# Second feed-forward part of an attention kernel as seven block products instead of eight

## The chip, the core and the metric

One core of a Trainium2 chip runs the whole program in one launch. The metric is the device time of that core in microseconds; the median of several runs counts. TensorE (PE in the profile) does the matrix products and accumulates them in PSUM, which has eight banks of 128 partitions by 512 float32. VectorE (DVE), ScalarE (ACT) and GpSimd (POOL) do the elementwise work, and SyncE (SP) issues every DMA. An engine works through its own instructions in order and waits for the others by semaphores.

## The reference, cut to what matters

```python
attn_out = _attn_ref(q, k, v, f)            # 4 batches, 8 heads, 576 tokens, head size 64
x = attn_out.transpose(0, 2, 1, 3).reshape(2304, 512)
x = square(maximum(x @ moe_w_in, 0)) @ moe_w_out         # first part:  512 -> 2048 -> 512
h = x @ moe2_w_in                                        # second part: 512 -> 2048
return (h - tanh(h)) @ moe2_w_out                        #              2048 -> 512
```

The attention has a causal mask and a decay. The weights arrive as float64 and are joined to float32 on the chip.

## The kernel before, in words

Attention and the first feed-forward part are interleaved on TensorE; the second part follows alone. All products of the feed-forward parts run on values split in two: a rounded high part in fp32r and a low part, the rest. One product of A and B is then three matmuls: high by high, low by high, high by low. A high part is a copy on ScalarE (`rounded`, L86), a low part a subtraction (`rest`, L100).

The first part goes through eight blocks of 288 tokens (TB, L48). For each of 16 feature tiles i, `h_step` (L131) does 12 matmuls (3 terms, 4 pieces of the contraction) into a bank, ScalarE applies Relu and two squares, and the low part is formed by the engine that the table ENG names (L155). `y_step` (L158) follows LAG = 2 steps later with 12 matmuls into four banks that hold the output of a block over all 16 steps. `y_out` (L697) splits the four banks into high and low, and stores both to y_d in DRAM (L75).

The second part uses the same two functions with ph = 2 on blocks of 512 tokens (TB2, L49): four of 512 and one of 256 (BLK, L728). Per step: 12 matmuls of 512 columns, Tanh on ScalarE (L152), the difference on DVE (L153), the high part on ScalarE (L154), the low part on DVE (L155), then 12 matmuls of `y_step`. `load_x` (L730) fetches a block's high and low from y_d, `out_emit` (L716) copies the result out of PSUM and stores it. `h_step` has one bank (psh, L172) until the last two blocks of the first part, when attention is over; from there it has three (psh2, L780).

Weights of the second part: `fetch_w` (L106) loads a half tile (512 KB as float64), `split_w` (L113) joins the two words on ScalarE and DVE (L120 to L122) and splits into high and low. `w2_split` (L762) spreads the 32 half tiles over the last two blocks of the first part and the first blocks of the second (W2_AT, L750). High and low then stay in SBUF; nothing of the weights goes back to DRAM. GpSimd has no work in this stretch.

The order of the instructions: the program is built twice. In the first stretch, up to MARK (block 2 of the first part, L771), each engine keeps the order of the first build (L815 to L823). Behind it the order comes from a scheduler that takes instructions by simulated time. The main loop is L769 to L812.

Of the kernel before, what the change touches and what calls it, by code (L numbers as in the profile page):

```python
# [48 lines left out]
TB2 = 512  # L49
# [4 lines left out]
def kernel(  # L54
# [76 lines left out]
    def h_step(ph, i, x, psh, n, j):  # L131
        xh, xl = x
        wh, wl = (W[ph, i, 0][:, a] for a in range(2))
        ps = psh.tile([128, 512], F32, tag="h", name="hp")[:, :n]
        ops = [(w, x, k) for w, x in ((wh, xh), (wl, xh), (wh, xl)) for k in range(NK)]
        for jj, (w, x, k) in enumerate(ops):
            xk = x[:, k] if ph == 1 else x[k // 2][:, k % 2]
            nc.tensor.matmul(ps, w[:, k * 128:(k + 1) * 128], xk, start=(jj == 0), stop=(jj == 11))  # L138
        if ph == 1:
            tmp = f1.tile([128, TB], F32, tag="tmp", bufs=2, name="tmp")  # L140
            gh = f1.tile([128, TB], F32R, tag="gh", bufs=RING, name="gh")
            gl = f1.tile([128, TB], F32R, tag="gl", bufs=RING, name="gl")
        else:
            tmp = late.tile([128, TB2], F32, tag="tmp", name="tmp", bufs=2)[:, :n]
            ghl = f1.tile([128, 4 * TB], F32R, tag="xhl", bufs=4, name="ghl")
            gh, gl = ghl[:, :n], ghl[:, TB2:TB2 + n]
        if ph == 1:
            nc.scalar.activation(tmp, ps, AF.Relu)  # L148
            nc.scalar.activation(gh, tmp, AF.Square)  # L149
            nc.scalar.activation(tmp, tmp, AF.Square)  # L150
        else:
            nc.scalar.activation(tmp, ps, AF.Tanh)  # L152
            nc.vector.tensor_tensor(tmp, ps, tmp, ALU.subtract)  # L153
            rounded(nc.scalar, gh, tmp)  # L154
        rest(by("gl7" if j == NB - 1 else "gl" if j < 2 else "l_gl") if ph == 1 else nc.vector, gl, tmp, gh)  # L155
# [717 lines left out]
```

## Time and profile before

| what | us |
|---|---|
| median of 3 runs | 1088.02 (1087.4 to 1090.89) |
| span of the profiled execution, first to last instruction | 1079.7 |
| TensorE busy | 1029.2 |
| VectorE busy | 594.0 |
| ScalarE busy | 524.7 |
| GpSimd busy | 250.6 |

The profile gives the profiled execution by its span; a time of its own beside it is not listed. Median less span is 8.3 us, the time around the program. Busy time of TensorE is modelled: neighbouring matmuls overlap, so the mean of one matmul (some 300 ns) is longer than the distance from one start to the next, and it is the distance that adds up to the time. "PEld" is TensorE's weight load, one for each matmul. A windows row gives, for a stretch, its length, the busy time and the number of instructions of each engine, the granted clock of TensorE, the busy share of the DMA engines and their rate.

### The profile page before, as it was taken

What the parts mean: (1) busy time and instruction counts of PE and PEld (TensorE: products, weight loads), DVE (VectorE), ACT (ScalarE), POOL (GpSimd) and SP (SyncE); (2) the same over time, 40 slices, a digit from 0 to 9 for tenths busy, and PEclk for the clock granted to TensorE, in tenths of its full rate; (3) what the DMA queues carried; (4) which work ended last, traced back from release to release, by engine and by line L of the source; (5) the groups of instructions that cost most, each with busy time, mean ns of one, the idle gap of its engine ahead of it and who ended that gap; (6) DMA issues with size and microseconds to landing.
All of it is one profiled execution on the core that took longest, in us unless ns stands there. A gap on an engine that the chain in (4) does not pass through costs nothing.

```text
span 1079.7 us, 16821 instructions
## 1 busy us (share of the span) xinstructions
PE 1029.2 (95%) x6048; PEld 898.8 (83%) x6048; DVE 594.0 (55%) x1566; ACT 524.7 (49%) x1221; POOL 250.6 (23%) x358
## 2 busy tenths in 40 slices
PE   4899999999999898999999999999999999999998
PEld 3577678888998888888889999888888888888898
DVE  5887777768787767877525545642222322222232
ACT  6977677665556446455436667432222222222232
POOL 4244455555353442534210000000000000000000
PEclk9989999999999899999989999999999999999999
DMA  7657643225955658745646088100200300110010
GB/s 243 199 138 213 185 140 136 89 82 174 293 180 171 195 154 253 258 141 162 184 161 228 2 305 285 45 1 25 92 1 1 117 1 1 39 40 1 1 40 21
DMA packets 63301, 134.83 MB, mean 125 GB/s; under 512 B 6416, under 2 KB 31568, under 8 KB 61168
## 3 DMA queue, kind: packets, MB, share of 16 engines
q1 hardware_dynamic: 63216, 133.74, 38.9%
q8 instruction: 48, 0.79, 0.3%
q14 instruction: 37, 0.30, 0.1%
HBM read 93.94 MB, written 39.78 MB: 124 GB/s over the span
## 4 chain that ended last, share of the span: by engine, by line
PE 75%; DMA 11%; DVE 6%; POOL 2%; issue 2%; SPq 2%; ACT 2%; POOLq 0%; ACTq 0%; DVEq 0%
PE hp L138 32%; PE yp L164 32%; DMA PTl<-p_d 6%; PE o_ps L552 3%; DMA p_d<-T 3%; PE o_ps L367 2%; DVE PTl L101 2%; PE s_ps L476 1%; SPq L518 1%; DVE P L443 1%; PE s_ps L477 1%; DMA raw<-in_w_dram 1%; POOL PTh L90 1%; PE s_ps L326 1%; PE t_ps L487 1%
## 5 line engine op out<-in xcount | busy, mean ns | idle before, releaser
L138 PE MATMUL hp<-xhl,w 128*128 128x288 f32 (+2 forms) x2496 | 454.2, 329 | 2.5 <-ACT tmp L148 1.7
L138 PEld LDWEIGHTS hp<-xhl,w 128*128 128x128 f32 x2496 | 388.8, 192 | 41.0 <-issue 2.7
L164 PE MATMUL yp<-ghl,w 128*128 128x512 f32 (+1 forms) x960 | 216.0, 374 | 0.0
L164 PE MATMUL yp<-gh,w 128*128 128x288 f32 x1024 | 200.9, 301 | 0.0
L164 PEld LDWEIGHTS yp<-ghl,w 128*128 128x128 f32 x960 | 168.4, 188 | 34.5
L153 DVE TENSOR_TENSOR tmp<-hp,tmp 128x512 f32<-128x512 f32 (+1 forms) x80 | 51.0, 638 | 209.8 <-ACT tmp L152 209.8
L164 PEld LDWEIGHTS yp<-gh,w 128*128 128x128 f32 x1024 | 161.9, 191 | 1.6 <-issue 0.4
L152 ACT ACTIVATE tmp<-hp 128x512 f32<-128x512 f32 (+1 forms) x80 | 44.4, 555 | 225.0 <-PE hp L138 224.8
L164 PE MATMUL yp<-gl,w 128*128 128x288 f32 x512 | 133.5, 299 | 2.6 <-DVE gl L101 1.5
L148 ACT ACTIVATE tmp<-hp 128x288 f32<-128x288 f32 x128 | 51.9, 407 | 121.6 <-PE hp L138 118.4
L452 ACT ACTIVATE P<-P,ST 128x320 f32<-128x320 f32 (+4 forms) x151 | 84.6, 561 | 39.5 <-DVE ST L443 38.2
L164 PEld LDWEIGHTS yp<-gl,w 128*128 128x128 f32 x512 | 90.4, 190 | 5.0 <-DVE gl L101 2.3
L463 POOL TENSOR_SCALAR P<-P,ST 128x448 f32<-128x448 f32 (+4 forms) x88 | 58.4, 666 | 93.3 <-DVE ST L457 52.3
L101 DVE TENSOR_TENSOR ghl<-tmp,ghl 128x512 fp32r<-128x512 f32 (+1 forms) x80 | 51.1, 639 | 49.2 <-ACT ghl L88 49.2
L443 DVE CUSTOM_DVE_ANT_0 P<-s_ps,mk 128x320 f32<-128x320 f32 (+3 forms) x151 | 63.6, 433 | 25.2 <-PE s_ps L477 12.0
L101 DVE TENSOR_TENSOR gl<-tmp,gh 128x288 fp32r<-128x288 f32 x96 | 48.4, 505 | 47.2 <-ACT tmp L150 46.6
L101 DVE TENSOR_TENSOR PTl<-PTl,PTh 128x512 fp32r<-128x512 f32 (+1 forms) x64 | 51.9, 841 | 39.4 <-POOL PTh L90 39.3
L88 ACT ACTIVATE ghl<-tmp 128x512 fp32r<-128x512 f32 (+1 forms) x80 | 47.2, 590 | 49.9 <-DVE tmp L153 49.8
L101 DVE TENSOR_TENSOR w<-wst,w 128x512 fp32r<-128x512 f32 x64 | 46.1, 725 | 28.9 <-ACT w L88 28.6
L90 POOL TENSOR_SCALAR PTh<-PTl 128x512 fp32r<-128x512 f32 (+1 forms) x64 | 46.3, 750 | 59.8 <-DMA PTl<-p_d 59.0
L149 ACT ACTIVATE gh<-tmp 128x288 fp32r<-128x288 f32 x128 | 56.5, 443 | 4.1 <-PE yp L164 1.2
L150 ACT ACTIVATE tmp<-tmp 128x288 f32<-128x288 f32 x128 | 56.0, 438 | 2.1
(122 smaller groups left out, 1187.7 us busy)
## 6 DMA issues: line engine op xcount, KB each, us to landing
raw<-in_w_dram SPq DMA_DIRECT2D x64, 512.0 KB
p_d<-T SPq DMA_DIRECT2D x16, 1024.0 KB
PTl<-p_d SPq DMA_DIRECT2D x64, 256.0 KB
R<-in_qk_dram SPq DMA_DIRECT2D x24, 576.0 KB
xhl<-y_d SPq DMA_DIRECT2D x16, 512.0 KB
xhl<-x_d SPq DMA_DIRECT2D x14, 576.0 KB
y_d<-yst SPq DMA_DIRECT2D x14, 576.0 KB
VR<-in_v_dram SPq DMA_DIRECT2D x32, 160.0 KB
```

Of the source, the lines that this page charges most:

```text
L88: eng.activation(out, in_, AF.Copy)
L90: eng.tensor_scalar(out, in_, 1.0, 1.0, ALU.mult, ALU.mult)
L101: eng.tensor_tensor(out, in_, hi.bitcast(F32), ALU.subtract)
L138: nc.tensor.matmul(ps, w[:, k * 128:(k + 1) * 128], xk, start=(jj == 0), stop=(jj == 11))
L148: nc.scalar.activation(tmp, ps, AF.Relu)
L149: nc.scalar.activation(gh, tmp, AF.Square)
L150: nc.scalar.activation(tmp, tmp, AF.Square)
L153: nc.vector.tensor_tensor(tmp, ps, tmp, ALU.subtract)
L164: nc.tensor.matmul(yp[m][:, :n], w[:, c], x, start=(i == 0 and j == 0), stop=(i == NF - 1 and j == 2))
L443: nc.vector.tensor_tensor_reduce(p[:rows, a:b], ps[:rows, :b - a], mk[:rows, o:o + b - a], -0.125, 3.0e38 if mn is None else mn, ALU.add, ...
L452: nc.scalar.activation(p[:rows, :n], p[:rows, :n], AF.Exp, bias=mn, scale=-1.0, accum_out=st[:rows, 1, t:t + 1])
L463: by(n_by).tensor_scalar(p[:rows, :n], p[:rows, :n], st[:rows, 3, t:t + 1], 1.0, ALU.mult, ALU.mult)
```

## The change

The second part is cut into 2 by 2 blocks and done by Strassen's scheme: seven products P1 to P7 of sums of blocks instead of eight products of blocks. The sums of the weights (S1 to S4) and of the activations (T1 to T4) are formed on DVE, split in high and low, and each of the seven products is again three matmuls.

- **h products.** A group g is two feature tiles (8 groups); a batch b is 576 tokens as two halves of 288 (N2). The loop of 32 steps n does P6, P1, P7, P5 of step n, then P2, P4, P3 of step n-1: 42 matmuls of 288 columns. Partial sums are formed in place: DVE adds to banks in PSUM, and P2, P4 and P3 accumulate on what is there. Four Tanh and four differences per step, one of the differences on GpSimd ("c22"). The result g_d goes to DRAM as float32 (590 KB a step).
- **y products.** Four rounds of 512 tokens. In each the seven accumulators stay in seven banks over all eight groups: 42 matmuls of 256 columns a group. `y_evict` combines the seven once a round, on DVE. The last 256 tokens go by the plain eight products (`y_rest`, 192 matmuls of 256 columns).
- **Weights.** `prep_all` joins, sums and splits a group's w_in (s = 0) during the last two blocks of the first part, at the steps PREPS, and stores high and low of seven blocks to wg_d in DRAM (1.84 MB a group; groups 6 and 7 stay in SBUF). `w_load` brings them back. w_out (s = 1) is prepared during the h loop (PREP2_AT). Low parts of w2 ("w2_lo") and of the h products' operands ("xo_lo") are on GpSimd; those of the y products stay on DVE.
- **Memory.** Weights of the first part move to pools that are closed one after another in its last block, and the new pools pa0 to pa3 open in their place. In the last two blocks `h_step` keeps the single bank psh; psh2 now belongs to the second part. `y_out` only copies out of PSUM, two banks on ScalarE and two on DVE, and y_d holds one float32 in place of two.
- **Order.** Everything of the second part is chained in the order in which it is written, on each engine.

```diff
--- before.py
+++ after.py
+    "w2_lo": "P", "xo_lo": "P", "c22": "P",
...
-TB2 = 512
+NG = NF // 2
+N2 = 288
+NQ = 256
+NYB = NTOK // (2 * NQ)
+PREPS = (((6, 1), 0, 0), ((6, 3), 0, 1), ((6, 6), 0, 2), ((6, 8), 0, 3), ((6, 11), 0, 4), ((6, 13), 0, 5),
+         ((7, 1), 1, 0), ((7, 6), 0, 6), ((7, 10), 0, 7))
+PREP2_AT = (None, 2, 6, 10, 14, 18, 25, 28)
+DIRECT = {(0, 6): 0, (0, 7): 1, (1, 6): 4, (1, 7): 6}
+HOME_G = ({6: 0, 7: 1, 0: 2, 1: 3, 2: 4, 3: 5, 4: 6, 5: 7}, {0: 2, 1: 3, 6: 4, 2: 5, 7: 6, 3: 7, 4: 0, 5: 1})
+YSEQ = (0, 6, 1, 7, 2, 3, 4, 5)
...
+    y_d = dram.tile([NK, 128, NTOK], F32, name="y_d")
+    g_d = [dram.tile([128, 2, NTOK], F32, name=f"g_d{g}") for g in range(NG)]
+    wg_d = [[dram.tile([128, 2, 7 + s, 256], F32, name=f"wg_d{s}_{g}") for g in range(NG)] for s in range(2)]
...
+    def prep_fetch(s, g):
+        raw = WRAW[s, g] = late.tile([128, 2, 1024], U32 if WIDE else F32, tag="raw", name="raw")
+        for n, a in enumerate(((1, 0), (0, 1))[s]):
+            src = w2[2 * g + a][:, s * 512:(s + 1) * 512]
+            nc.sync.dma_start(raw[:, n] if WIDE else raw[:, n, :512], src.bitcast(U32) if WIDE else src)
...
+    def prep_sum(s, g, name):
+        q = {k: WT[s, g][:, i] for k, i in (SLOT[s] | SUMS).items()}
+        a, b, op = WSUM[name]
+        nc.vector.tensor_tensor(q[name], q[a], q[b], op)
...
+    def prep_lo(s, g, a, b):
...
+        t = WT[s, g][:, a:b]
+        rest(by("w2_lo"), t, t, WH[s, g][:, a:b])
...
+        src = WT[s, g] if which else WH[s, g].bitcast(F32)
+        o = 1 - s
+        nc.sync.dma_start(wg_d[s][g][:, which, a - o:b - o], src[:, a:b])
...
+    def prep_all(s, g):
+        with tc.issue_after(latest(EngineType.DVE)):
+            for n in range(2):
+                prep_wide(s, g, n)
+                prep_shift(s, g, n)
+                prep_or(s, g, n)
+            for k in ("S1", "S3", "S2", "S4"):
+                prep_sum(s, g, k)
+            cuts_ = (1 - s, 2, 4, 6, 8)
+            for a, b in zip(cuts_, cuts_[1:]):
+                prep_hi(s, g, a, b)
+                prep_lo(s, g, a, b)
+            for which in range(2):
+                prep_store(s, g, which, 1 - s, 8)
...
+    def w_load(s, g):
+        hl = home(s, g)
...
+            nc.sync.dma_start(hl[:, a].bitcast(F32), wg_d[s][g][:, a, s:])
+        place(s, g, hl)
...
+    def x_op(b, names):
+        for n in names:
+            xo = x_out(b, n)
+            rounded(nc.scalar, xo[:, 0], XT[b, n])
+            rest(by("xo_lo"), xo[:, 1], XT[b, n], xo[:, 0])
...
+                psh2 = ctx.enter_context(tc.tile_pool(name="psh2", bufs=1, space=bass.MemoryType.PSUM))
...
+                G[g] = h_step(i, X[j], psh, TB, j)
+            for k, (at, *which) in enumerate(PREPS):
+                if (j, i) == at:
+                    prep_all(*which)
+                    prep_fetch(*(PREPS[k + 1][1:] if k + 1 < len(PREPS) else (1, 1)))
...
+        if jy == NB - 1 and iy % 4 == 3 and iy < 15:
+            early[iy // 4].close()
+            pa.append(ctx.enter_context(tc.tile_pool(name=f"pa{iy // 4}", bufs=1)))
+            if iy == 3:
+                x_load(0)
+                x_sum(0, ("T1", "T2", "T3", "T4"))
+            elif iy == 7:
+                x_op(0, ("T2", "B11", "T3", "T1", "B21", "T4", "B22"))
+            else:
+                w_load(0, 0)
+                w_load(0, 1)
...
+    TERMS = ((0, 0), (1, 0), (0, 1))
+    FACTORS = {"P1": ("A11", "B11"), "P2": ("A12", "B21"), "P3": ("S4", "B22"), "P4": ("A22", "T4"),
+               "P5": ("S1", "T1"), "P6": ("S2", "T2"), "P7": ("S3", "T3")}
+    HOME = {"P1": 0, "P2": 0, "P6": 1, "P7": 2, "P4": 2, "P5": 3, "P3": 3}
+    RING7 = [(0, i) for i in (1, 2, 3)] + [(1, i) for i in range(4)]
...
+    def h_prod(n, p):
+        b, g = divmod(n, NG)
+        wn, xn = FACTORS[p]
+        wg, xo = WG[0, g][wn], XO[b, xn]
+        ps = BK[n][HOME[p]]
+        first_ = p in ("P6", "P1", "P7", "P5")
+        for i, (ws, xs, k) in enumerate([(ws, xs, k) for ws, xs in TERMS for k in range(2)]):
+            nc.tensor.matmul(ps, wg[:, ws, k * 128:(k + 1) * 128], xo[:, xs, k],
+                             start=(i == 0 and first_), stop=(i == 5), skip_group_check=True)
+    def h_act(n, k):
+        src = BK[n][(0, 2, 3)[k]]
+        q = (1, 3, 0)[k]
+        nc.scalar.activation(TH[:, k], src, AF.Tanh)
+        nc.vector.tensor_tensor(GQ[n][:, q], src, TH[:, k], ALU.subtract)
...
+    def y_sum(n):
+        if n >= REST:
+            return
+        B12, B11, B22, B21, T1, T2, T3, T4 = (GT[n][:, i] for i in range(8))
+        for o, x, y in ((T1, B12, B11), (T3, B22, B12), (T2, B22, T1), (T4, B21, T2)):
...
+        rounded(nc.scalar, YO[n][0], GT[n][:, 8 - q:])
...
+        rest(nc.vector, YO[n][1], GT.pop(n)[:, 8 - q:], YO[n][0])
...
+    YORDER = ("P1", "P6", "P2", "P7", "P4", "P5", "P3")
+    def y_prod(n, p, acc):
+        i, g = n % NG, YSEQ[n % NG]
+        wn, xn = FACTORS[p]
+        wg = WG[1, g][wn]
+        for m in range(2):
+            ps = acc[p][:, m * NQ:(m + 1) * NQ]
+            for j, (ws, xs) in enumerate(TERMS):
+                nc.tensor.matmul(ps, wg[:, ws, m * 128:(m + 1) * 128], YO[n][xs][:, YX[xn]],
+                                 start=(j == 0 and m == 0 and i == 0), stop=(j == 2 and i == NG - 1), skip_group_check=True)
...
+        nc.scalar.activation(cp, v["P1"], AF.Copy)
+        add(u2, v["P6"], cp)
+        add(o1[:, :, 1], v["P2"], cp)
+        add(x, v["P7"], u2)
+        add(o2[:, :, 1], v["P4"], x)
+        add(z, v["P5"], u2)
+        add(o2[:, :, 0], v["P5"], x)
+        nc.sync.dma_start(out[0:2, :, t:t + 2 * NQ].rearrange("k p n -> p k n"), o2.rearrange("p m a n -> p m (a n)"))
+        add(o1[:, :, 0], v["P3"], z)
+        nc.sync.dma_start(out[2:4, :, t:t + 2 * NQ].rearrange("k p n -> p k n"), o1.rearrange("p m a n -> p m (a n)"))
...
+    XOP_AT = {4: ("B11",), 6: ("T2",), 7: ("B21",)}
+    TSUM_AT = {4: ("T1", "T3"), 5: ("T2", "T4")}
+    YLOAD_AT = {25: 0, 26: 1, 28: 2, 30: 3, 31: 4}
...
+        x = [bank2(*RING7[(3 * n + i) % 7])[:, :N2] for i in range(3)]
+        BK[n] = [x[0], bank2(0, 0)[:, :N2], x[1], x[2]]
...
+        if n < 3:
+            w_load(0, n + 3)
+        if g == 3 and b + 1 < B:
+            x_load(b + 1)
...
+        for p in ("P6", "P1", "P7", "P5"):
+            h_prod(n, p)
+        nc.scalar.activation(cp, BK[n][0], AF.Copy)
+        nc.vector.tensor_tensor(uv, BK[n][1], cp, ALU.add)
+        if g == NG - 1 and b + 1 < B:
+            x_op(b + 1, ("T3",))
+        nc.vector.tensor_tensor(BK[n][2], BK[n][2], uv, ALU.add)
...
+        nc.vector.tensor_tensor(c22, BK[n][3], xc, ALU.add)
+        nc.vector.tensor_tensor(BK[n][3], BK[n][3], uv, ALU.add)
...
+            GQ[n - 1] = late.tile([128, 4, N2], F32, tag="gq", bufs=2, name="gq")
+            h_prod(n - 1, "P2")
+            h_act(n - 1, 0)
...
+            nc.scalar.activation(TH[:, 3], SM[:, 6 + (n - 1) % 2], AF.Tanh)
+            by("c22").tensor_tensor(GQ[n - 1][:, 2], SM[:, 6 + (n - 1) % 2], TH[:, 3], ALU.subtract)
+            h_prod(n - 1, "P4")
+            h_act(n - 1, 1)
+            h_prod(n - 1, "P3")
+            h_act(n - 1, 2)
...
+                prep_hi(1, k, 0, 4)
+                prep_lo(1, k, 0, 2)
+                prep_lo(1, k, 2, 4)
...
+            h_store(n - 1)
...
+    for n in range(REST):
+        k, g = divmod(n, NG)
+        if g == 0:
+            if k:
+                keys, spare_key = [spare_key] + keys[:-1], keys[-1]
+            acc = {p: bank2(*key) for p, key in zip(YORDER, keys)}
+        for p in YORDER:
+            y_prod(n, p, acc)
+        y_load(n + 4)
+        if n == 1:
+            w_load(1, 5)
+        if n == 0:
...
+        y_rest(u, acc)
...
```

## Rows read from the trace of the kernel before

**Rows 1.** The page: span, busy time by engine, chain by engine and by line.

```profile
span 1079.7 us, 16821 instructions
PE 1029.2 (95%) x6048; PEld 898.8 (83%) x6048; DVE 594.0 (55%) x1566; ACT 524.7 (49%) x1221; POOL 250.6 (23%) x358
...
PE 75%; DMA 11%; DVE 6%; POOL 2%; issue 2%; SPq 2%; ACT 2%; POOLq 0%; ACTq 0%; DVEq 0%
```

**Rows 2.** Windows: the first part's last two blocks; from the first 512-column matmul on.

```profile
565.00:669.75 104.75, 104.75 (x790) 104.75 (x788) 54.20 (x107) 69.00 (x158) 0.00 (x0) 1.00 0.60 212
669.75:1079.70 409.95, 405.89 (x1946) 337.68 (x1944) 127.34 (x206) 109.37 (x194) 0.00 (x0) 1.00 0.08 29
```

**Rows 3.** Timeline of PE: start, length of the group, matmul, count; 512 columns.

```profile
669.75 2.93 PE L138 MATMUL hp<-xhl,w 128*128 128x512 f32 x12
...
689.55 2.92 PE L138 MATMUL hp<-xhl,w 128*128 128x512 f32 x12
...
695.12 2.92 PE L138 MATMUL hp<-xhl,w 128*128 128x512 f32 x12
```

**Rows 4.** Timeline of PE: 288 columns, with 12 of y_step between the two.

```profile
663.36 1.76 PE L138 MATMUL hp<-xhl,w 128*128 128x288 f32 x12
...
666.55 1.76 PE L138 MATMUL hp<-xhl,w 128*128 128x288 f32 x12
```

**Rows 5.** Timeline of PE: 256 columns, 276 matmuls from the first start to the last group's.

```profile
1038.12 1.59 PE L138 MATMUL hp<-xhl,w 128*128 128x256 f32 x12
...
1071.15 4.48 PE L164 MATMUL yp<-ghl,w 128*128 128x256 f32 x36
```

**Rows 6.** Groups by form: count, busy us, mean ns of one, idle time before.

```profile
L138 PE MATMUL hp<-xhl,w 128*128 128x288 f32 x1536 | 241.4, 304 | 2.5 <-ACT tmp L148 1.7 <-ACT xs L88 0.6
...
L120 ACT ACTIVATE wst<-raw 128x512 f32<-128x512 f32 x64 | 42.5, 669 | 18.2 <-DMA raw<-in_w_dram 11.6 <-DVE w L101 6.5
L88 ACT ACTIVATE w<-wst 128x512 fp32r<-128x512 f32 x64 | 39.8, 625 | 23.1 <-DVE wst L122 23.1
L148 ACT ACTIVATE tmp<-hp 128x288 f32<-128x288 f32 x128 | 51.9, 407 | 121.6 <-PE hp L138 118.4 <-POOL ST L241 1.4 <-DVE gl L101 0.8
...
L88 ACT ACTIVATE xsh<-xs 128x576 fp32r<-128x576 f32 x8 | 5.4, 679 | 4.8 <-DVE xs L564 4.8
...
L122 DVE SCALAR_TENSOR_TENSOR wst<-wst 128x512 uint32<-128x512 uint32 x64 | 45.5, 715 | 4.9 <-ACT wst L120 3.0
...
L121 DVE TENSOR_SCALAR wst<-raw 128x512 uint32<-128x512 uint32 x64 | 30.7, 483 | 6.5 <-DMA raw<-in_w_dram 6.4
...
L101 DVE TENSOR_TENSOR yst<-yp,yst 128x288 fp32r<-128x288 f32 x32 | 13.2, 442 | 3.3 <-ACT yst L88 3.3
...
L101 DVE TENSOR_TENSOR ghl<-tmp,ghl 128x512 fp32r<-128x512 f32 x64 | 44.3, 692 | 41.9 <-ACT ghl L88 41.9
...
L101 DVE TENSOR_TENSOR ghl<-tmp,ghl 128x256 fp32r<-128x256 f32 x16 | 6.8, 425 | 7.3 <-ACT ghl L88 7.3
...
L101 POOL TENSOR_TENSOR gl<-tmp,gh 128x288 fp32r<-128x288 f32 x32 | 28.9, 902 | 27.6 <-ACT tmp L150 23.2 <-issue 4.3
...
L101 POOL TENSOR_TENSOR xs<-xs,xsh 128x576 f32<-128x576 f32 x12 | 17.5, 1459 | 15.7 <-ACT xsh L88 15.4
...
L101 POOL TENSOR_TENSOR VH<-VR,VH 128x256 fp32r<-128x256 f32 x16 | 11.8, 738 | 46.0 <-ACT VH L88 46.0
```

**Rows 7.** Timeline of DVE and POOL: the same subtraction alone, and beside GpSimd's.

```profile
295.50 0.45 DVE L101 TENSOR_TENSOR gl<-tmp,gh 128x288 fp32r<-128x288 f32 x1
...
299.74 0.99 DVE L101 TENSOR_TENSOR gl<-tmp,gh 128x288 fp32r<-128x288 f32 x1
...
298.38 2.03 POOL L101 TENSOR_TENSOR QB<-R,QA 64x576 fp32r<-64x576 f32 x1
```

**Rows 8.** Windows in which the DMA engines were full.

```profile
275.00:285.00 10.00, 10.00 (x77) 9.99 (x77) 8.79 (x29) 7.34 (x21) 5.19 (x8) 1.00 1.06 278
630.00:640.00 10.00, 10.00 (x77) 10.00 (x77) 3.76 (x7) 4.58 (x11) 0.00 (x0) 1.00 0.99 332
640.00:650.00 10.00, 10.00 (x77) 10.00 (x76) 6.41 (x13) 8.72 (x20) 0.00 (x0) 1.00 0.99 386
```

More of the change, by code (lines that the diff above doesn't have):

```diff
@@ L128, in split_w, with h_step @@
         W[ph, i, s] = hl
-    def h_step(ph, i, x, psh, n, j):
+    def h_step(i, x, psh, n, j):
         xh, xl = x
-        wh, wl = (W[ph, i, 0][:, a] for a in range(2))
+        wh, wl = (W[1, i, 0][:, a] for a in range(2))
         ps = psh.tile([128, 512], F32, tag="h", name="hp")[:, :n]
@@ L136, in h_step, with y_step @@
         for jj, (w, x, k) in enumerate(ops):
[L137 to L155, printed above, removed]
+            nc.tensor.matmul(ps, w[:, k * 128:(k + 1) * 128], x[:, k], start=(jj == 0), stop=(jj == 11))
+        tmp = f1.tile([128, TB], F32, tag="tmp", bufs=2, name="tmp")
+        gh = f1.tile([128, TB], F32R, tag="gh", bufs=RING, name="gh")
+        gl = f1.tile([128, TB], F32R, tag="gl", bufs=RING, name="gl")
+        nc.scalar.activation(tmp, ps, AF.Relu)
+        nc.scalar.activation(gh, tmp, AF.Square)
+        nc.scalar.activation(tmp, tmp, AF.Square)
+        rest(by("gl7" if j == NB - 1 else "gl" if j < 2 else "l_gl"), gl, tmp, gh)
         return gh, gl
-    def y_step(ph, i, g, yp, n):
+    def y_step(i, g, yp, n, at):
         gh, gl = g
-        wh, wl = (W[ph, i, 1][:, a] for a in range(2))
+        wh, wl = (W[1, i, 1][:, a] for a in range(2))
         for m in range(NK):
@@ new lines, with prep_tile @@
+    WIDE = w2.dtype == I64
+    KEPT = {}
+    BUFS = {(0, k): ("xo0", "xo1") if k % 2 == 0 else ("wt", "hi") for k in range(6)}
+    BUFS |= {(1, 0): ("xo0", "xo1"), (0, 6): ("wt", None), (0, 7): ("hi", None)}
+    def prep_tile(s, g, which, dtype):
+        if s and g:
+            if which not in KEPT:
+                KEPT[which] = late.tile([128, 8, 256], dtype, tag=("wt", "hi")[which], name=("wt", "whi")[which])
+            return KEPT[which]
+        return late.tile([128, 8, 256], dtype, tag=BUFS[s, g][which], name=("wt", "whi")[which])
@@ new lines @@
+    n = NSTEP - 1
+    GQ[n] = late.tile([128, 4, N2], F32, tag="gq", bufs=2, name="gq")
+    h_prod(n, "P2")
+    h_act(n, 0)
+    nc.scalar.activation(TH[:, 3], SM[:, 6 + n % 2], AF.Tanh)
+    by("c22").tensor_tensor(GQ[n][:, 2], SM[:, 6 + n % 2], TH[:, 3], ALU.subtract)
+    h_prod(n, "P4")
+    h_act(n, 1)
+    h_prod(n, "P3")
+    h_act(n, 2)
+    h_store(n)
+    y_hi(1)
+    y_lo(1)
+    y_sum(2)
+    y_load(3)
+    keys = [(0, 0)] + [RING7[i] for i in (5, 6, 0, 1, 2, 3)]
+    spare_key = RING7[4]
@@ new lines @@
+    acc = [bank2(*keys[0]), bank2(*spare_key)]
+    for u in range(2):
+        y_rest(u, acc)
+    t = 2 * NQ * NYB
+    for o, eng in ((1, nc.scalar), (0, nc.vector)):
+        x = late.tile([128, 2, NQ], F32, tag="gq", bufs=2, name="yo")
+        src = acc[o].rearrange("p (m n) -> p m n", m=2)
+        if eng is nc.scalar:
+            eng.activation(x, src, AF.Copy)
+        else:
+            eng.tensor_copy(x, src)
+        nc.sync.dma_start(out[2 * o:2 * o + 2, :, t:].rearrange("k p n -> p k n"), x)
@@ L817 @@
+    emitted = list(nc.cur_bb.bb.instructions)
+    by_name = {x.name: x for x in emitted}
     same_order = mybir.DependencyInfo(mybir.DependencyClass.NoSync, mybir.DependencyReason.DATA)
-    for name in order:
-        if name in first_part:
-            ins = by_name[name]
+    for chain in ([by_name[n] for n in order if n in first_part], [x for x in emitted if x.name not in second_part]):
+        last = {}
+        for ins in chain:
             if ins.engine in last:
```

353 lines of the change are left out of this document (271 added, 82 removed), and 2 rows, old and new, of the table ENG.

## The prediction

> **What bounds the kernel now.** I read the page first, for who is busy and who is on the chain that ended last: TensorE is busy 95% of the span and makes up 75% of the chain; DVE stands at 55%, ScalarE at 49%, GpSimd at 23% [rows 1]. Such shares are means over stages, so the windows come next. In the last two blocks of the first part TensorE is busy for all of 104.75 us, and from the first 512-column matmul to the last it never waits: 405.89 us busy, the rest of that window being the store at the end. GpSimd does nothing in either stretch, and the DMA engines are at 0.60 and then 0.08 of their time [rows 2]. So the second part, 38% of the span, lasts as long as its matmuls take, and the question is what one matmul costs at each width. That is read from starts in the timeline, not from the mean duration, since matmuls overlap.
>
> - 512 columns: 689.55 to 695.12 us is 24 matmuls, 232 ns each [rows 3].
> - 288 columns: 663.36 to 666.55 us is 24 matmuls, 132.9 ns each [rows 4].
> - 256 columns: 1038.12 to 1071.15 us is 276 matmuls, 119.7 ns each [rows 5].
>
> The granted clock is 1.00 in these stretches, the level of 2.4 GHz [rows 2]; columns alone then take 213, 120 and 107 ns, and a matmul costs some 13 to 19 ns more. Cutting columns therefore pays nearly in full, and narrower matmuls lose little.
>
> **Matmuls out and in.** Out: from 669.75 us to the end of the last matmul at 1071.15 + 4.48 = 1075.6 us [rows 3, 5] is 405.9 us, of which 24 matmuls of 288 columns (3.2 us) belong to the first part and stay: 402.7 us. From counts: 1536 x 232 ns + 384 x 119.7 ns = 402.3 us, the same. In: 32 steps of 42 matmuls of 288 columns, 1344 x 132.9 ns = 178.6 us; 32 group steps of 42 plus 192 of 256 columns, 1536 x 119.7 ns = 183.9 us; together 362.5 us. TensorE's own saving is 40.2 us. It is under an eighth of 402.7 because the narrow matmuls carry the fixed 13 ns more often (2880 for 1920) and the last 256 tokens keep eight products.
>
> In the 288-column stretch PEld is busy throughout, at 512 columns 82% [rows 2]. If weight loads set the pace, 256 columns could not be quicker than 288; they are, 119.7 against 132.9 ns [rows 4, 5], so columns set it, and I keep 183.9 us. The Trainium skill (Perfetto Trace Analysis, Identifying the Most-Contended Engine) takes the busy share of weight loads as TensorE's measure of how near it is to its limit; by that the 256-column matmuls would also cost 132.9 ns, 20.3 us more. The trace disagrees at 256 columns.
>
> **What else must fit beside it.** One h step is 42 x 132.9 ns = 5.58 us. Over 32 steps, 178.6 us:
>
> - DVE: seven operations of 288 columns with a PSUM operand a step. The trace has none that writes to PSUM in place; from below 0.3 us (the columns alone at about 1 ns each, from 692 - 425 ns for 256 more), from above a 512-column operation's 692 ns; I take 442 ns, the same width [rows 6], so 99 us. Seven weight groups, each two shifts (483), two joins (715) and four sums of 256 columns (425): 4.1 us, 29 us. Twelve sums of 576 columns at 760 ns (the line through 425 and 692): 9 us. Sum 137 us; at the 692 ns bound 193 us, above TensorE's 178.6.
> - ScalarE: six copies and Tanh a step at 407 ns, 78 us; seven groups at two joins (669) and four copies' worth (625), 3.8 us, 27 us; 21 copies of 576 columns at 679 ns, 14 us. Sum 119 us [rows 6].
> - GpSimd: 32 differences at 902 ns, 29 us; seven groups of four low parts of 512 columns, 1.32 us each by the line through 738 and 1459, 37 us; 21 low parts of 576 columns at 1459 ns, 31 us [rows 6]. Sum 97 us.
>
> All three fit on average. A product's chain (copy of P1, add to P6, add into P7, copy, two adds) takes some 3 us and has until P4 of the same step, 42 matmuls later, so a late operation of 1 or 2 us is covered; without that cover it would cost its own length in each step. In a y step, 42 x 119.7 ns = 5.03 us, DVE has four sums (425) and a low part of 1792 columns (2.0 us), 3.7 us, plus seven adds of 692 ns a round; ScalarE 1.7 us. Each add frees its bank ahead of the next round's product for it. I cost the rounds at 0, bound 3 us; the cover is the spare eighth bank.
>
> GpSimd now works where it was idle, and it slows DVE: the subtraction that takes 0.45 us alone took 0.99 us beside a GpSimd subtraction [rows 7]. It concerns DVE operations with both operands in SBUF, here the weight groups and the 576-column sums, 38 us of the h loop. Doubled, DVE has 175 of 178.6 us. The Trainium skill (SBUF — State Buffer, Who interferes with whom) says why: such an operation and a GpSimd one that reads SBUF take turns at a port, the later one waiting for all of the other. By that rule 68 DVE operations, each behind a whole 1.32 us, would come to 90 us; the row shows a wait of about half a microsecond.
>
> **Where time is given back.**
>
> - *Last two blocks of the first part.* `h_step` keeps one bank, so the next h product waits for Relu, with 12 matmuls (1.6 us) to cover it. ScalarE gets 9 weight groups (33 us) and 7 copies, 79 us of 104.75 in place of 69.00 [rows 2]; a copy of 0.6 us ahead of Relu still fits, two or a wait for DVE do not. With one bank in the six blocks before, such waits summed to 1.7 us [rows 6]; from above 0.5 us in each of 32 steps, 16 us. I take 4 us, nearer to the row.
> - *Start of the h loop.* The first weights (two groups, 3.7 MB) can be loaded only when the last block's twelfth step has freed their place, some 72 matmuls (9.6 us) ahead of the loop. At 332 to 386 GB/s [rows 8] the first group needs 5 to 6 us and the second as much again. I take 2 us, bounds 0 and 8.
> - *h loop.* SP's queue now carries the store of g_d (590 KB a step), stores and loads of prepared weights, and x: 18.9 + 11.0 + 6.3 + 16.5 + 3.5 + 1.6 = 57.8 MB. In 178.6 us that is 323 GB/s, where the trace's full windows show 278 to 386 [rows 8]. A stalled store holds `gq` (two buffers), so DVE's differences, then the banks, then TensorE. There are about 10 us of cover; loads bunch at steps 0 to 5 and 25 to 31. I take 4 us, bounds 0 and 29 (57.8 MB at 278 GB/s is 208 us).
> - *From h to y.* The last group's low parts on GpSimd free the buffer of the second y operand. I take 2 us, bounds 0 and 5.
> - *`y_out`.* It loses DVE subtractions in six blocks beside attention; I count 0, bounds 3 us either way, since the scheduler will order that stretch anew. The end differs by two evictions of 512 columns for 256, 0.3 us.
>
> Sum: -40.2 + 4 + 2 + 4 + 2 + 0.3 = -27.9 us. The trace's 1079.7 us becomes 1051.8; with the 8.3 us between span and median, 1088.0 becomes 1060.1. I say 1060.
>
> **Rivals.**
>
> 1. *The last two blocks stall.* One bank and a crowded ScalarE queue, 0.5 to 1 us in most of 32 steps: 24 in place of 4 us, 1080. For it: DVE and DMA delays now reach ScalarE's queue; 7 fetches and 6 stores (18 MB) fall into 51 us. Against: 1.7 us before with one bank [rows 6].
> 2. *DVE becomes the bound of the h loop*, through GpSimd's port or dear operations into PSUM: 193 us instead of 178.6, so 14 more, 1074.
> 3. *DMA becomes the bound and the change is slower.* From the weight groups to the end of the h loop there are 90 MB (32 and 57.8) for 283 us of matmuls, 318 GB/s. At 278 GB/s it takes 324 us and the gain is gone, 1088. Below that it is a loss: at 250 GB/s 360 us, 77 more than the matmuls, 1125. Against: 278 was seen with the transposes' small packets; w2's fetches, like the new rows of 1 KB and more, ran at 386 [rows 8].
> 4. *Weight loads set 256 columns at 132.9 ns*: 1080. The trace speaks against it.
>
> **How the numbers follow.** Forecast 0.66; rivals 1 to 4: 0.12, 0.10, 0.09, 0.03. All but the third are faster; of its 0.09 I give 0.06 to slower and 0.03 to no change, and 0.02 and 0.01 more for the same ends reached by stalls added up. So faster 0.88, same 0.04, slower 0.08; 0.3% (3 us) is what a measurement here tells from no change. The range goes from 1045 (no stall, and 3 us gained beside attention) to 1083, which takes in rivals 1, 2 and 4 and leaves out the third.
>
> **What would show it.** Right: h steps 5.6 us and y steps 5.0 us apart, granted clock 1.00, PE idle of some 10 us between the start of the weight groups and the end. Wrong: h steps well over 6 us (with DVE near 100%: rival 2; with the DMA share near 1 and differences waiting for g_d: rival 3), h products waiting for Relu in the last two blocks (rival 1), y matmuls 133 ns apart (rival 4).

## The result, and the profile after

| | median us | runs | ratio to before (95% interval) |
|---|---|---|---|
| before | 1086.64 | 13 | |
| the change | 1073.51 | 13 | 0.9884 (0.9856 to 0.9913) |

The change gains 13.1 us of the median, where 27.9 were forecast; 1073.5 lies in the range of 1045 to 1083. The direction was right and the size was not. One reading ahead of the result has to be put right: the 8.3 us between the median and the span before are not the time around the program. An execution's time lies 1.8 us above its own span (1073.96 and 1072.2 us with the change; 1088.65 and 1086.8 us in a second profile of the kernel before), so the first profiled execution of the kernel before was a quick one. The forecast was taken off the median and is not touched by it. The page of the changed kernel, its first and fourth part and a group that matters:

```profile
span 1072.2 us, 19736 instructions
PE 994.2 (93%) x7008; PEld 925.1 (86%) x7008; DVE 756.4 (71%) x1843; ACT 586.1 (55%) x1314; POOL 405.5 (38%) x484
...
PE 58%; DMA 16%; DVE 14%; ACT 4%; issue 4%; POOL 2%; SPq 2%; POOLq 0%; DVEq 0%; ACTq 0%
...
L173 PE MATMUL yp<-gl,w 128*128 128x288 f32 x512 | 116.7, 301 | 12.1 <-DVE gl L117 9.3
```

Against [rows 1] TensorE is busy 35 us less, DVE 162 us more, and TensorE's share of the chain falls from 75 to 58%: the second part no longer runs by matmuls alone. Its new idle time is in the first part too, where y waits for gl. The windows that answer to [rows 2]: the last two blocks of the first part, the h loop, the y part.

```profile
572.94:690.86 117.92, 109.20 (x798) 107.23 (x797) 73.53 (x115) 72.69 (x162) 55.88 (x43) 0.99 0.72 253
690.86:878.31 187.45, 180.96 (x1331) 178.71 (x1329) 141.71 (x294) 104.94 (x241) 95.77 (x80) 0.99 0.79 296
878.31:1072.20 193.89, 185.76 (x1538) 184.57 (x1536) 134.41 (x191) 60.63 (x43) 5.21 (x3) 1.00 0.47 151
```

The busy times of the three other engines are close to what was worked out (DVE 142 for 137, ScalarE 105 for 119, GpSimd 96 for 97 us in the loop). And the matmuls cost what was said. In the timeline of PE, steps of the middle of the h loop, and of the y part:

```profile
765.27 4.96 PE L969 MATMUL wp<-xo,wg 128*128 128x288 f32 x36
770.07 0.96 PE L969 MATMUL wp<-xs,wg 128*128 128x288 f32 x6
770.86 4.96 PE L969 MATMUL wp<-xo,wg 128*128 128x288 f32 x36
...
949.78 20.44 PE L1045 MATMUL wp<-go,wg 128*128 128x256 f32 x169
```

From 765.27 to 770.86 us is one step of 42 matmuls, 133.1 ns each, as in [rows 4]; 169 matmuls of 256 columns in 20.3 us (the last one's overlap taken off) are 120.0 ns each, as in [rows 5]. So the saving of TensorE's own work is there, and what went wrong is what was given back:

| stretch | forecast given back, us | measured, us |
|---|---|---|
| last two blocks of the first part | 4 | 12.1 |
| h loop (start 2, loop 4) | 6 | 11.0 |
| to y and y part | 2.3 | 6.2 |
| sum | 12.3 | 29.3 |

What is measured here is a stretch's loss: its length less its matmuls at 132.9 and 119.7 ns each. The first stretch runs from the first h matmul of block 6 to the end of the last y matmul of block 7: 117.9 us for 796 matmuls (105.8 us; before 112.5 us for 804 and 24 of 512 columns, 112.4 us). The loop and the y part are 189.6 and 190.1 us for 178.6 and 183.9. 40.2 - 29.3 = 10.9 us; 24 of y's matmuls that stood behind the start of block 6 now stand ahead of it, 3.2 us; so 14.1 from block 6 on, where the two profiles differ by 14.3 (509.7 and 495.4 us to the last matmul) and the medians by 13.1. The second profile of the kernel before took 511.1 us there, 1.4 more, all of it in the last two blocks; differences of that size between single executions tell nothing. Who made TensorE wait there (the waits of PE from 573 us on: line, who for, us in total, times, longest):

```profile
PE yp L173 <- DVE gl L117: 7.1, 5, 3.4
PE wp L1045 <- DVE go L117: 3.3, 2, 1.7
PE wp L969 <- DMA wg<-wg_d: 2.4, 1, 2.4
PE wp L969 <- DVE gq L976: 2.1, 2, 1.6
PE hp L157 <- ACT tmp L161: 1.5, 1, 1.5
PE wp L969 <- ACT sm L1103: 1.2, 1, 1.2
```

The largest is DVE's subtraction gl, which feeds y in the first part. The timeline around the longest of these waits, of all engines:

```profile
654.80 0.74 DVE L866 TENSOR_TENSOR xa<-xa 128x576 f32<-128x576 f32 x1
655.14 5.06 POOL L117 TENSOR_TENSOR xo<-xa,xo 128x576 fp32r<-128x576 f32 x3 [0.55 <-ACT xo L104]
655.47 1.89 DVE L780 SCALAR_TENSOR_TENSOR wt<-wx,wt 128x512 uint32<-128x512 uint32 x1
...
657.28 1.66 DVE L117 TENSOR_TENSOR gl<-tmp,gh 128x288 fp32r<-128x288 f32 x1
...
658.86 3.51 DVE L785 TENSOR_TENSOR wt<-wt 128x256 f32<-128x256 f32 x3
658.99 1.23 PE L173 MATMUL yp<-gl,w 128*128 128x288 f32 x4 [3.35 <-DVE gl L117]
```

While GpSimd runs three low parts of 576 columns, DVE does the join of 0.7 us in 1.89, gl of 0.45 in 1.66 and sums of 0.42 in 1.2 each; PE stands for 3.35 us. The granted clock then falls, here and after the wait at the start of the loop (windows of PE's clock, the third number from the end):

```profile
655.00:660.00 5.00, 1.65 (x9) 1.41 (x8) 5.00 (x4) 3.03 (x7) 4.86 (x3) 0.91 0.57 195
660.00:665.00 5.00, 3.95 (x21) 3.72 (x20) 2.33 (x3) 3.06 (x6) 3.97 (x4) 0.75 0.00 0
700.00:705.00 5.00, 4.64 (x24) 4.64 (x25) 1.23 (x3) 0.62 (x2) 0.00 (x0) 0.66 1.01 426
```

0.66 and 0.75 are means over both levels, 1.2 and 2.4 GHz; in the last window 24 matmuls took what 35 take at full clock, so the 2.4 us wait cost 4 us in all in this execution (not in every one, see the end).

### The profile page after: what moved, and what is told of

It is laid out like the page before. It is cut to its first block, busy times and chain, and to the rows that moved or that the text cites. A ratio compares the mean times of both kernels' runs of the same rounds, so it can differ in the third digit from the quotient of the medians.

```text
span 1072.2 us, 19736 instructions
## 1 busy us (share of the span) xinstructions
PE 994.2 (93%) x7008; PEld 925.1 (86%) x7008; DVE 756.4 (71%) x1843; ACT 586.1 (55%) x1314; POOL 405.5 (38%) x484
## 4 chain that ended last, share of the span: by engine, by line
PE 58%; DMA 16%; DVE 14%; ACT 4%; issue 4%; POOL 2%; SPq 2%; POOLq 0%; DVEq 0%; ACTq 0%
PE wp L1045 15%; PE wp L969 13%; PE hp L157 9%; PE yp L173 8%; DMA PTl<-p_d 7%; PE o_ps L559 3%; DMA raw<-in_w_dram 3%; DMA p_d<-T 2%; PE wp L1057 2%; DVE PTl L117 2%; PE o_ps L374 2%; SPq L525 1%; DMA R<-in_qk_dram 1%; DVE P L450 1%; DVE gl L117 1%
## 5 line engine op out<-in xcount | busy, mean ns | idle before, releaser
L157 PE MATMUL hp<-xhl,w 128*128 128x288 f32 x1536 | 238.2, 301 | 7.1 <-ACT tmp L161 6.2
L157 PEld LDWEIGHTS hp<-xhl,w 128*128 128x128 f32 x1536 | 216.9, 192 | 13.6 <-ACT tmp L161 8.0
L969 PE MATMUL wp<-xo,wg 128*128 128x288 f32 x1152 | 162.4, 298 | 6.5 <-DMA wg<-wg_d 2.4
L1045 PE MATMUL wp<-go,wg 128*128 128x256 f32 x1344 | 162.7, 283 | 4.3 <-DVE go L117 3.3
L1045 PEld LDWEIGHTS wp<-go,wg 128*128 128x128 f32 x1344 | 161.7, 192 | 5.3 <-DVE go L117 4.1
L969 PEld LDWEIGHTS wp<-xo,wg 128*128 128x128 f32 x1152 | 156.9, 190 | 8.7 <-DVE gq L976 2.9
L173 PE MATMUL yp<-gl,w 128*128 128x288 f32 x512 | 116.7, 301 | 12.1 <-DVE gl L117 9.3
L104 ACT ACTIVATE go<-gt 128x1792 fp32r<-128x1792 f32 (+1 forms) x34 | 58.3, 1717 | 108.0 <-PE wp L1045 62.0
L173 PEld LDWEIGHTS yp<-gl,w 128*128 128x128 f32 x512 | 84.0, 189 | 16.8 <-DVE gl L117 13.1
L117 DVE TENSOR_TENSOR go<-gt,go 128x1792 fp32r<-128x1792 f32 (+1 forms) x34 | 69.3, 2038 | 27.6 <-ACT go L104 24.3
L117 POOL TENSOR_TENSOR wt<-wt,whi 128x512 f32<-128x512 f32 (+1 forms) x48 | 63.9, 1352 | 61.3 <-ACT whi L104 50.4
L1020 DVE TENSOR_TENSOR gt<-gt 128x256 f32<-128x256 f32 x128 | 53.4, 458 | 9.4 <-DMA gt<-g_d 8.3
```

Source lines behind the costliest of these rows:

```text
L104: eng.activation(out, in_, AF.Copy)
L117: eng.tensor_tensor(out, in_, hi.bitcast(F32), ALU.subtract)
L157: nc.tensor.matmul(ps, w[:, k * 128:(k + 1) * 128], x[:, k], start=(jj == 0), stop=(jj == 11))
L173: nc.tensor.matmul(yp[m][:, :n], w[:, c], x, start=(at == 0 and j == 0), stop=(at == NF - 1 and j == 2))
L969: nc.tensor.matmul(ps, wg[:, ws, k * 128:(k + 1) * 128], xo[:, xs, k], start=(i == 0 and first_), stop=(i == 5), skip_group_check=True)
L1020: nc.vector.tensor_tensor(o, x, y, ALU.subtract)
```

## The experiments

**Low parts ahead of the loop on DVE.** The theory: GpSimd's low parts hold up DVE and so gl. Rivals: the single h bank with Relu behind ScalarE's copies; late DMAs.

```diff
-        rest(by("w2_lo"), t, t, WH[s, g][:, a:b])
+        rest(by("w2_lo" if s and g else "w2_lo0"), t, t, WH[s, g][:, a:b])
...
-            rest(by("xo_lo"), xo[:, 1], XT[b, n], xo[:, 0])
+            rest(by("xo_lo" if b else "xo_lo0"), xo[:, 1], XT[b, n], xo[:, 0])
```

with "w2_lo0" and "xo_lo0" on DVE.

> All low parts that are formed ahead of the h loop (nine weight groups and the seven operands of the first batch, 43 operations, about 57 us of GpSimd) go to DVE; those inside the loop stay on GpSimd. The stretch from the first h matmul of the first part's block 6 to the last y matmul of block 7 took 117.8 us with the change and 106.9 us before. Theory A (GpSimd holds up DVE's subtraction gl, and gl holds up y): though DVE gets 28 us more work, gl is back at 0.45 us and the stretch falls to 107 to 111 us, the run by some 8 us against the changed kernel (ratio to before about 0.981). Theory B (one bank, Relu behind ScalarE's copies): nothing changes for ScalarE, the stretch stays above 115 us. Theory C (DMA late): the same as B.

Measured: 1064.76 us, ratio 0.9803 (0.9766 to 0.9839). The stretch of the two blocks, here and below taken to the start of its last matmul, is 107.5 us for 117.8, its loss 1.9 us for 12.1. All executions of gl in it, first with the change, then here (min/median/max ns):

```profile
L117 DVE TENSOR_TENSOR gl<-tmp,gh x33: 444/459/1655, 572.9 to 687.2; 128x288 fp32r<-128x288 f32 x33
```

```profile
L117 DVE TENSOR_TENSOR gl<-tmp,gh x33: 447/454/462, 574.7 to 678.6; 128x288 fp32r<-128x288 f32 x33
```

Not one gl is held up any more, though DVE was given 43 operations more, and PE's waits for gl fall from 7.1 us to this:

```profile
PE yp L173 <- DVE gl L117: 0.3, 1, 0.3
```

In that stretch DVE's busy time did not even grow: 73.68 us here for 73.53 in the rows above. What GpSimd took off DVE, its hold on DVE gave back. The single bank and the DMA are as before in this run, so neither of the two rivals costs much without the hold.

**Three banks for h in the last two blocks.**

```diff
-        ps = psh.tile([128, 512], F32, tag="h", name="hp")[:, :n]
+        pool, tag = (psh2, f"p{1 + (j * NF + i) % 3}") if j >= NB - 2 else (psh, "h")
+        ps = pool.tile([128, 512], F32, tag=tag, name="hp")[:, :n]
```

> In the last two blocks of the first part the h product goes round three banks again, as before the change; nothing else differs. Theory B (one bank): the stretch of these two blocks falls from 117.8 us to under 111. Theory A (GpSimd and DVE): it stays within 2 us of 117.8, since it was y that waited for gl (about 8 us with its followers) and h for Relu only once, 1.5 us.

Measured: 1061.70 us, ratio 0.9771 (0.974 to 0.9802); the stretch is 113.3 us and holds 24 matmuls more, its loss 4.4 us for 12.1. Neither theory had it: the bank is worth 7.7 us there, without gl being quicker (up to 1681 ns). The waits of PE in the stretch:

```profile
PE yp L174 <- DVE gl L117: 2.6, 1, 2.6
```

The place of y goes with it. The timeline of PE with the change, an h product and the first use of its gl, one step behind:

```profile
646.49 1.76 PE L157 MATMUL hp<-xhl,w 128*128 128x288 f32 x12
...
652.31 0.70 PE L173 MATMUL yp<-gl,w 128*128 128x288 f32 x4
```

and with three banks, where y stands two steps behind:

```profile
640.45 1.76 PE L158 MATMUL hp<-xhl,w 128*128 128x288 f32 x12
...
648.72 0.29 PE L174 MATMUL yp<-gl,w 128*128 128x288 f32 x1
```

From the end of the h product gl has 4.1 us in the first and 6.5 in the second, which is also its time before the change:

```profile
589.86 1.76 PE L138 MATMUL hp<-xhl,w 128*128 128x288 f32 x12
...
598.12 0.30 PE L164 MATMUL yp<-gl,w 128*128 128x288 f32 x1
```

gl is done 1.9 us after the product when nothing is in its way. With the change it takes more than 4.1 us in nine of the 32 steps and more than 6.5 in two. The scheduler chose the earlier place when h had one bank; the two runs differ in nothing else. So the single bank cost little by Relu (1.5 us, once), the mechanism that the prediction looked at, and took away the cover of another chain. No run kept the one bank with the later place of y, so that the place, and not the bank as such, is what counts is argued from these times and from the waits.

**GpSimd's low parts in halves.**

```diff
-                prep_lo(s, g, a, b)
+                for c in range(a, b):
+                    prep_lo(s, g, c, c + 1)
```

and the first batch's operands likewise.

> GpSimd's low parts ahead of the h loop are cut to half their length (256 columns for 512, 288 columns times one for 576), the work is the same. Theory A in the form that a DVE operation waits for the whole of the GpSimd operation that came first: gl beside GpSimd takes up to 0.45 + 0.8 = 1.25 us in place of up to 1.66, and the stretch falls by 2 to 5 us though GpSimd is busy about 10% longer. Theory A in the form that the two share a port in proportion: the slowdown of DVE stays as it is or grows, the stretch stays at 117 to 120 us. Theories B and C: no change.

Measured: 1074.15 us, ratio 0.9904 (0.9868 to 0.9941); the stretch is 116.7 us and its loss 11.0 for 12.1, less than the 2 to 5 us expected. Of gl, and of PE's waits in the stretch:

```profile
L117 DVE TENSOR_TENSOR gl<-tmp,gh x33: 443/493/1060, 573.9 to 686.9; 128x288 fp32r<-128x288 f32 x33
...
PE hp L157 <- ACT tmp L161: 4.6, 5, 3.1
PE yp L173 <- DVE gl L117: 1.0, 2, 0.7
```

The longest gl falls from 1655 to 1060 ns, about by the half of GpSimd's operation that is gone. That fits a wait for the end of the operation that came first and not a sharing in proportion. The waits for gl nearly go too, but Relu is now late in their place, so the time hardly moves: this run tells the form of the hold, and is inconclusive on its price. Why Relu came late was not followed up.

**The kernel before once more.**

> The kernel before once more, for a second profile of it. The part beside attention, up to the first h matmul of block 6, took 565.9 us in its first profile and 572.9 us with the change. If those 7 us are the scatter of single executions, this profile lies anywhere from 563 to 574; if the new order of that stretch costs them, it lies at 566 again, and the kernels of this call that keep the change at 571 to 574.

Measured: 571.7 us to block 6, and a span of 1086.8. So the 7 us by which the two first profiles differ ahead of block 6 are scatter of single executions: 565.9 and 571.7 before, 563.9 to 575.4 in the kernels with the change. Single executions are therefore compared by stretches, not by their whole length.

**Both edits together.**

> Both edits of the first call together: low parts ahead of the loop on DVE, three banks for h in the last two blocks. If GpSimd and the single bank are two faces of one chain (a late gl holds up y, and with one bank the next h cannot go ahead of it), the second edit adds little: the stretch of blocks 6 and 7 is 106.8 to 107.5 us, against 107.5 with the first edit alone and 113.3 with the second alone. If they are two separate costs they add, and the stretch cannot go under the 106.8 us of its matmuls either, so the two readings differ only in PE's idle time there: 1.1 us stays, or goes to 0.

Measured: 1058.84 us, ratio 0.9752 (0.9708 to 0.9797), 26.7 us under before. The stretch:

```profile
568.60:677.50 108.90, 108.90 (x821) 108.90 (x821) 74.25 (x159) 74.52 (x170) 0.00 (x0) 1.00 0.74 272
```

TensorE never waits in it, and its loss is 0. The stretch is 1.4 us longer than with the first edit alone, because it holds 24 matmuls more (820 for 796, 3.2 us) and loses 1.9 us less; that is why it is outside the expected 106.8 to 107.5. The edits gave 10.2 and 7.7 us singly and 12.1 together. As no more than 12.1 could be had, the sum does not tell one chain from two. What speaks for one chain, gl's time and gl's cover, is that both edits take away the same wait: y for gl, 7.1 us, is 0.3 with the first and 2.6 with the second. By the sign that was set beforehand, idle time at 0, the banks also remove a small cost of their own, at most 1.9 us.

**Fewer loads at the end of the h loop.** Left of the loss were the ends of the loop and the start of y. Near the end of the loop of the changed kernel the DMA engines are full:

```profile
850.00:855.00 5.00, 5.00 (x40) 5.00 (x38) 2.75 (x6) 3.50 (x8) 2.72 (x3) 1.00 1.03 401
```

```diff
-    YLOAD_AT = {25: 0, 26: 1, 28: 2, 30: 3, 31: 4}
+    YLOAD_AT = {25: 0, 28: 1}
...
-        if n == 1:
-            w_load(1, 5)
+        if n < 4:
+            w_load(1, n + 2)
```

> Of the five loads of prepared w_out that bunch at the end of the h loop (steps 25, 26, 28, 30, 31) only two stay there (steps 25 and 28); three move into the first y steps. Theory D (the DMA engines are full from 845 to 875 us, the store of g_d comes late, its buffer gq holds up DVE and GpSimd, and so PE): waits for the landing of g_d fall from 10.8 us to under 3, PE's idle time in the h loop from 6.5 to about 3.5 us, the loop from 189.6 to 186 us. Rival E (DVE's sums of the first y steps wait behind GpSimd's low parts at the loop's end): no change of the loop by more than 1 us.

Measured: 1076.26 us in a single execution. The wait at step 30 went (that step's matmuls were 178 ns apart and are 133.5), but the waits for the landing of g_d still sum to 10.6 us, and the loop is 188.3 us and not 186, since steps 6 and 17 lost as much (167 and 149 ns a matmul). But those two steps lie ahead of every load that was moved, and in the other runs they range from 133 to 182 and from 133 to 148, so this is scatter and not the edit's price. The y part rose from 190.1 to 193.7: the values of g_d for its steps 6 to 8 came late beside the moved loads, with the DMA engines full (401 to 414 GB/s from 900 to 915 us). What left the loop came back behind it.

**Loads one step later at the start, the last group's low parts on DVE at the end.**

```diff
-        if n < 3:
-            w_load(0, n + 3)
+        if 1 <= n < 4:
+            w_load(0, n + 2)
```

and "w2_lo" of the last group (1, 7) on DVE.

> Two edits at two ends. At the start of the h loop the loads of the weights of groups 3 to 5 are written one step later, so that group 2 shares the DMA engines with one load in place of two: the wait for wg_d of 2.4 us at the third step falls under 1 us, and the granted clock stays 1.00 there (0.66 with the change, 5 us long, worth 1.5 us). At the end the last weight group's low parts go from GpSimd to DVE: under theory E DVE's 256-column sums there are back from about 1.0 to 0.42 us, and PE's idle time in the y part falls from 4.3 us to under 2; under theory D the y part keeps its idle time.

Measured: 1078.78 us in a single execution. Both expectations on TensorE's waits failed, though DVE's sums of 256 columns are back at 0.41 to 0.43 us as theory E had it.

```profile
PE wp L1045 <- DVE go L117: 3.8, 1, 3.8
PE wp L969 <- DVE gq L976: 3.5, 4, 1.5
PE wp L969 <- DMA wg<-wg_d: 2.6, 1, 2.6
```

The third group's weights are late by themselves: their load can start only with the pool that opens after the last y matmul, at 691 us, and was needed at 698. At the start of y three waits became one of 3.8 us.

**No GpSimd in the second part.**

```diff
-    "w2_lo": "P", "xo_lo": "P", "c22": "P",
+    "w2_lo": "V", "xo_lo": "V", "c22": "V",
```

> GpSimd gets no work in the second part: all low parts and the fourth difference on DVE. Ahead of the loop the stretch of blocks 6 and 7 is at 107 to 108 us, as with the first edit of the first call. In the loop DVE gets 50 us more, 175 to 190 of 179 us: if GpSimd's help is worth more than its hold on DVE, the loop gets longer than 189.6 us, by up to 10 us; if the hold costs as much as the help gives, it stays at 186 to 191 us.

Measured: 1066.26 us in a single execution; 106.9 us for the two blocks (loss 1.3), 192.5 for the loop. The window of the loop:

```profile
679.40:869.80 190.40, 181.78 (x1330) 177.42 (x1329) 162.26 (x373) 101.33 (x241) 0.00 (x0) 1.00 0.78 290
```

DVE has 162 us for 142, not the 175 to 190 expected, and the steps that carry x's operands run at 140 to 167 ns a matmul. The moved operations add up to 48 us on DVE, but its operations with all operands in SBUF, 55 us beside GpSimd, now take 38; most of DVE's operations there read PSUM, and those are not held up (below). In the loop GpSimd's help is worth about 3 us, or up to 5: with its work on GpSimd and the loads unchanged, five runs had loops of 187.2 to 189.6 us.

**First sums of y one step earlier, then also the loads spread.** On top of both edits together:

```diff
-        if n == NSTEP - 2:
-            y_sum(0)
-            y_hi(0)
-        if n == NSTEP - 1:
-            y_lo(0)
-            y_sum(1)
+        if n == NSTEP - 3:
+            y_sum(0)
+        if n == NSTEP - 2:
+            y_hi(0)
+            y_sum(1)
+        if n == NSTEP - 1:
+            y_lo(0)
```

> On top of the two edits of c2: the sums of the first two y steps are formed one loop step earlier, ahead of the last weight group's low parts on GpSimd. Theory E (at the loop's end those sums wait behind GpSimd, ScalarE's copy of them waits behind the sums, and the copy of P1 behind that): the sums take 0.42 us each in place of about 1.0, the last two loop steps fall from 165 and 185 ns a matmul to under 150, the loop from 187.2 to about 184.5 us, the y part from 190.1 to about 187. Theory D (the store of g_d, late because the DMA engines are full, is the first cause): both stay within 1 us of c2.

> As f1, and the loads of prepared w_out are spread over steps 25, 27, 29 and 31 and the first two y steps, a smaller shift than that of e5. If both theories hold for a part of the end, the wait for the landing of g_d at step 30 goes as in e5 (178 to 134 ns a matmul there) and, since the loads are only one or two steps later, no y step waits: loop and y part together 2 us below f1, ratio to before about 0.970. If the loads are as late as in e5, y steps 6 to 8 wait again and f2 is no faster than f1.

The second adds YLOAD_AT = {25: 0, 27: 1, 29: 2, 31: 3} and loads of groups 4 and 5 at y steps 0 and 1. Measured: 1057.26 us, 0.9730 (0.9686 to 0.9774), and 1055.49 us, 0.9709 (0.9677 to 0.9741). With the sums alone the last loop step falls from 165 to 137 ns a matmul, but the wait at step 30 stays (175). The loop is 188.5 us, not 184.5, and the y part 189.3, not 187: theory E explains little, and the fault at the end was first the late store of g_d. With both, every step from 10 on runs at 133 to 142 ns and every y step but the first at 120; the loop is 183.4 us. Idle time of the engines until g_d had landed, with the sums alone and with both (us, times):

```profile
  DMA g_d<-gq: 10.3, 4
```

```profile
  DMA g_d<-gq: 3.5, 4
```

The medians of the two differ by 1.8 us and their intervals overlap, so the gain of the second over the first is shown by the loop and not by the whole time. All waits of TensorE that are left from block 6 on:

```profile
PE wp L1046 <- DVE go L117: 3.2, 1, 3.2
PE wp L970 <- DMA wg<-wg_d: 2.5, 1, 2.5
```

This is the best version: 31.0 us under before, with an interval that ends at 0.9741, below the change's, which begins at 0.9856. What is left at the start of y was not taken further. The trace shows what it is: the low part of y's first operand, 1792 columns on DVE, 2.0 us alone and here 2.8 beside GpSimd. It begins 0.7 us after y's first matmul:

```profile
859.54 2.80 DVE L117 TENSOR_TENSOR go<-gt,go 128x1792 fp32r<-128x1792 f32 x1 [0.60 <-DMA wg_d<-whi]
```

## Why the prediction was right in direction and wrong in size

- **Matmuls out and in, 40.2 us.** Right: 133.1 and 120.0 ns measured for 132.9 and 119.7. In the best version, with every wait but two gone, 31.0 of the 40.2 arrive.
- **The rule on weight loads.** The matmuls of 256 columns keep 120.0 ns, so loads do not set the pace, and the fourth rival is out. The Trainium skill (Perfetto Trace Analysis, Identifying the Most-Contended Engine) judges TensorE's headroom by the busy share of weight loads, beside its rate of work. That share is 95% both in the h loop (178.71 of 187.45 us) and in the y part (184.57 of 193.89), at 133.1 and 120.0 ns a matmul: here it does not tell the pace.
- **The last two blocks, 4 us forecast, 12.1 measured. This is the step that failed**, with 8.1 of the 17.0 us given back beyond the forecast, in two places. First, GpSimd's hold on DVE stood at nothing here. The prediction let it concern "the weight groups and the 576-column sums, 38 us of the h loop" and left out gl, the very operation of [rows 7], which feeds y in these blocks; and it took one row for the price ("the row shows a wait of about half a microsecond"). In that row GpSimd's operation of 2.03 us had 0.67 us left when DVE's came, and DVE's took 0.54 us more than alone, so the row itself fits a wait for the end. In these blocks DVE operations of 0.42 to 0.69 us took up to 1.9. The Trainium skill (SBUF — State Buffer, Who interferes with whom) has the later operation wait for the whole of the earlier one; the run with halved operations agrees (1655 to 1060 ns), and the prediction set that rule aside. Second, the cover was reckoned for Relu alone ("a copy of 0.6 us ahead of Relu still fits"). The chain that broke was gl's, whose time shrank from 6.5 to 4.1 us when the single bank came with an earlier y. Moving GpSimd's work or giving back the banks each removes most of it, and both together all of it. The first rival foresaw a stall here, but of h behind Relu.
- **The h loop, 6 forecast, 11.0 measured**, a term under-sized with its mechanism right. Start: 4.05 us for 2, of which 2.4 is the wait and the rest the low clock after it. The wait is for the third group, whose place comes free only with the last y matmul; the first two, with which the prediction reckoned, came in time. Steps 6 to 9 lost about 2 us (0.1 to 3.3 in other runs with the same code there), the end about 4 us: the DMA engines are full there and the store of g_d holds gq, as foreseen. Spreading the loads, with the sums already early, took the end's part away. The third rival (slower by DMA) did not come about: over the whole loop the DMA engines were busy 0.79 of the time at 296 GB/s, and full ones moved 401 from 850 to 855 us, above the 278 to 386 of [rows 8].
- **To y and the y part, 2.3 forecast, 6.2 measured.** "The last group's low parts on GpSimd free the buffer" looked at one chain; DVE's sums behind GpSimd and ScalarE's copy waiting for them are in the trace too. But the runs that took GpSimd's last low parts or the sums out of the way still lost 7.4 and 5.4 us in the y part, and the best version 5.5. What stays in it is the low part of y's first operand, for which the prediction had no term. How the 6.2 us divide among these is open. The banks of the rounds cost nothing, as forecast.
- **DVE as the bound of the loop** (second rival): no. In-place additions in PSUM take 455 to 467 ns for the 442 assumed, and DVE has 142 us of the loop's 187. That 1073.5 lies next to this rival's 1074 is chance.

## What to carry to other kernels

Before giving an idle engine work, look not at its busy time but at what it makes another engine wait for, and price that wait by the longest operation it can stand behind. When a change takes a buffer or a bank away, follow every chain that used its slack, not only the one that reads it. A gain in an engine's own work is worth only what the two ends of the stretch let through: spread a burst of loads so that a small store whose buffer is needed next does not wait behind it.

## What the runs showed of the hardware

DVE operations with one operand in PSUM were not held up by GpSimd in any execution of these two lines. In the h loop of the changed kernel, with GpSimd busy half of the time (min/median/max ns):

```profile
L976 DVE TENSOR_TENSOR gq<-wp,sm x93: 440/450/461, 696.6 to 878.0; 128x288 f32<-128x288 f32 x93
L1107 DVE TENSOR_TENSOR wp<-wp,sm x32: 456/467/467, 691.4 to 875.5; 128x288 f32<-128x288 f32 x32
```

The same width from SBUF, gl above, went from 444 to 1655. So GpSimd's work was a help in one stretch and cost 10 us in another. A wait of PE of 2.4 us was followed by a granted clock of 0.66 over 5 us, which cost another 1.6 us. The same wait at the same step, 2.3 us long, was not followed by a lower clock in the run with both edits:

```profile
685.00:690.00 5.00, 2.67 (x21) 2.44 (x20) 1.21 (x3) 0.96 (x3) 0.81 (x1) 1.00 1.02 426
690.00:695.00 5.00, 5.00 (x39) 5.00 (x39) 3.89 (x9) 3.20 (x8) 1.34 (x1) 1.00 1.00 415
```

In the best version, after 2.5 us, it also stayed at 1.00; in the run with the sums alone, after 2.4 us, it fell to 0.66. So the length of a wait alone did not decide what the clock did.
